# Reordering the start-up of a fused attention and two-layer kernel: one load, one attention pass and one product moved

## The chip, the cores and the metric

The kernel runs on one core of a Trainium2 chip. The metric is the device time of one execution in microseconds (us), as the median of several executions. All times come from runs whose state is "fast" unless the text says otherwise. A profiled execution of the same program gives the "span", from the first to the last instruction, which is about 1.7 us shorter than the device time.

Engine names as in the profile: PE is TensorE's matmuls, DVE VectorE, ACT ScalarE, POOL GpSimd, SP SyncE (SPq: the transfers that it issues).

## The reference, cut to what matters

```python
# q, k, v: (4, 8, 768, 64) f32; n_sink 4, window 64; heads 0, 2, 6 "retrieval"
scores = scale * np.matmul(q, k.transpose(0, 1, 3, 2))
causal = rel >= 0
stream_keep = causal & (is_sink | in_win)          # the other five heads
mask = full causal for retrieval heads, stream_keep for the others
a = exp(scores - max) / sum
x = (a @ v) with heads side by side                # (3072, 512)
h = x @ w_in                                       # 512 x 2048   "product 1"
g = np.maximum(0.01 * h, h)
return (g @ w_out).astype(np.float32)              # 2048 x 512   "product 2"
```

## The kernel before

The 3,072 tokens are worked through in eight chunks of 384 (CH), numbered n = 0 to 7. A chunk is loaded (q, k and v, cast to bf16 on the way), its q and k are transposed ("prep"), attention makes x, product 1 makes g in 16 blocks of four matmuls each, product 2 makes three output tiles in 15 portions of two to four matmuls. Each stage is a list of small functions ("slots"), and `merge` weaves two lists together. PSUM is the buffer in which TensorE leaves its results; its banks are taken by a tag: `bank("py", ...)`. The tags psS, ph and po have two banks each, py and pt one.

```python
def load(n, nms="kqv"):                 # L93: GpSimd issues, one piece per group of 128 tokens
    ...
            cast[nm, n] = rot.tile([128, 3, H, D], BF16, name=f"{nm}b", tag=f"{nm}b", bufs=2)
    ...
            nc.gpsimd.dma_start(out=o, in_=nat[nm][b, c, :, :, g])

def prep_pair(n, p, tag="pt", eng=("v", "v", "v")):
    ...
    pt = bank(tag, [128, 2, 4, 128], BF16)          # k and q of two heads in ONE bank
    for e, nm in enumerate("kq"):
        for g in range(3):
            nc.tensor.transpose(pt[:, e, g, :], cast[nm, n][:, g, 2 * p : 2 * p + 2, :], ident[:])   # L201
    ... # move(): VectorE tensor_copy (L206) for "v", ScalarE activation Copy (L208) for "a"
    for hh in range(2):
        r = slice(64 * hh, 64 * hh + 64)
        move(eng[hh], kt[i][r, p, hh, CH * c : CH * c + CH], pt[r, 0, 0:3, :])
        ...
    move(eng[2], qts[n][:, p, :], pt[:, 1, 0:3, :])

def prep_dma(n):                        # chunks 3 to 7: transposes by DMA, issued by SyncE
    ...
        nc.sync.dma_start_transpose(out=kt..., in_=kz[n % 2][:, g]...)            # L223
        nc.sync.dma_start_transpose(out=qts[n][:, :, t], in_=cast["q", n][:, g]...)   # L225

# Attention: scores L329, exp on ScalarE L334, times v L296; x: VectorE L402, transposes L411,
# copy of the transposed x out of bank "pt" on ScalarE L412
def in_slots(n, tags=("ph",)):
    def tick(t):                        # one of 16 blocks
        ph = bank(tags[t % len(tags)], [128, 512], FP32)
        for g in range(KG):
            nc.tensor.matmul(ph[:, 0:CH], lhsT=w_in_bf[...], rhs=xts[n][:, g, :], ...)      # L457
        nc.scalar.activation(out=gs[n][:, t, :], in_=ph[:, 0:CH], func=ACTF.Prelu, alpha=0.01)   # L459
    ...
def out_slots(n, tags=("py", "py", "py"), halves=False):
    ...                                 # matmuls with w_out L470, VectorE copy to o L475, store L476
```

The part of the program that the change touches, in the kernel before:

```python
for i in range(4):
    load_w("in", i)
load(1)
...
for i in range(4):
    load_w("out", i)
...                                     # attention of chunk 0
load(2)
in0 = in_slots(0, ("ph", "psS"))
run(in0[0:12])
for p in range(4):
    prep_pair(1, p, ("py", "pt")[p % 2])
    run(in0[12 + p : 13 + p])
...
a1 = Attention(1, po_tags=("po", "po", "po", "ph")).slots(order=[0, 2, 6, 1, 3, 4, 5, 7])
run(a1[0:4])
run(merge(out_slots(0, ("py", "ph", "py")), a1[4:] + [lambda: None] * 3))
...
in1 = in_slots(1)
run(in1[0:1])
run(merge(in1[1:] + out_slots(1, ("py", "ph", "py")), preps(2) + Attention(2).slots()))
```

The softmax here doesn't subtract the row's maximum and nothing guards it: scores larger than these inputs give would overflow.

## Time and profile before

The time before is 248.32 us, the median of three runs (247.95 to 249.04). The profiled execution, a run apart (248.99 us), has a span of 247.3 us.

| moment, from the TensorE timeline of the kernel before | us |
|---|---|
| product 1 of chunk 0 starts | 19.57 |
| first transposes of chunk 1 (first prep) | 27.62 |
| fifth portion of product 2 of chunk 0, after a wait for w_out | 44.99 |
| product 1 of chunk 1 starts | 57.68 |
| product 1 of chunk 2 starts | 87.64 |
| end | 247.3 |

A row of a timeline reads: start, duration, engine, line and operation, result<-operands, how many in one group, and in brackets how long the engine had been idle before it and whose result it had waited for. The page's rows of digits are tenths of busy time in 40 slices of the span, some 6.2 us each. The lines themselves stand in the prediction.

### The profile page before, as it was taken

The page shows a single profiled execution, that of the slowest core. Times are in us where ns is not written, and L with a number is a line of the kernel's source. Part 1 is how long each engine was busy: PE and PEld are TensorE (multiplying, and loading weights), DVE is VectorE, ACT ScalarE, POOL GpSimd, SP SyncE. Part 2 cuts the span into 40 slices and gives each one's busy share as a digit, 9 for nine tenths or more (in the row PEclk, how much of TensorE's full clock was granted, in tenths as well). Part 3 has the DMA queues.
Part 4 walks back from the last instruction along what each step waited for, and adds up shares of the span by engine and source line. Part 5 has one row for each costly group of instructions (what it writes and reads, how often), then busy time and mean ns, then how long its engine had stood idle before and what let it go on. Part 6 is the DMA issues. An engine that isn't in the chain of part 4 may idle for free.

```text
span 247.3 us, 4993 instructions
## 1 busy us (share of the span) xinstructions
PE 226.4 (92%) x1984; PEld 136.7 (55%) x1984; DVE 92.2 (37%) x261; ACT 130.4 (53%) x280; POOL 80.3 (32%) x108
## 2 busy tenths in 40 slices
PE   1778698898799999999999999999999999999994
PEld 0565354464465566656655666566556665555553
DVE  6883065274725423444421334224411352111121
ACT  2676436553484289865536675366436764333300
POOL 8993772679493804842810000000000000000000
PEclk9999979999999999999999999999999999999999
DMA  9999999999999999999999642197301212111012
GB/s 162 137 158 199 155 197 231 157 188 165 167 147 178 176 193 174 158 127 158 172 137 172 129 104 74 25 154 176 96 16 42 62 29 64 42 42 45 28 57 85
DMA packets 114858, 30.78 MB, mean 124 GB/s; under 512 B 105620, under 2 KB 110996, under 8 KB 114836
## 3 DMA queue, kind: packets, MB, share of 16 engines
q0 software_dynamic: 78304, 13.51, 79.7%
q1 hardware_dynamic: 36432, 16.95, 33.8%
q8 instruction: 15, 0.25, 0.4%
q14 instruction: 7, 0.06, 0.1%
q10 hardware_dynamic: 100, 0.02, 0.1%
HBM read 27.81 MB, written 6.29 MB: 138 GB/s over the span
## 4 chain that ended last, share of the span: by engine, by line
PE 76%; DMA 11%; POOL 6%; DVE 4%; issue 1%; ACT 1%; POOLq 0%
PE ph L457 27%; PE py L470 21%; PE po L296 6%; DMA w_out_bf<-in_moe_w_out_dram 6%; PE pt L470 6%; DMA w_in_bf<-in_moe_w_in_dram 5%; PE psS L329 4%; PE psS L470 4%; PE ph L470 3%; PE psS L365 2%; POOL va L93 2%; PE psS L309 2%; DVE o L475 1%; POOL qb L93 1%; POOL w_out_bf L102 1%
## 5 line engine op out<-in xcount | busy, mean ns | idle before, releaser
L457 PE MATMUL ph<-xt,w_in_bf 128*128 128x384 bf16 x480 | 97.6, 327 | 0.1
L459 ACT ACTIVATE g<-ph 128x384 bf16<-128x384 f32 x120 | 59.0, 492 | 59.4 <-PE ph L457 59.0
L470 PE MATMUL py<-w_out_bf,g 128*128 128x512 bf16 (+1 forms) x256 | 66.4, 372 | 1.3 <-DMA w_out_bf<-in_moe_w_out_dram 0.7
L457 PEld LDWEIGHTS <-w_in_bf 128*128 128x128 bf16 x512 | 46.4, 98 | 30.1 <-issue 1.0
L470 PEld LDWEIGHTS <-g 128*128 128x128 bf16 x400 | 35.4, 97 | 27.6 <-issue 2.3
L334 ACT ACTIVATE at<-psS 128x384 bf16<-128x384 f32 x81 | 39.0, 490 | 16.6 <-PE psS L329 15.1
L86 POOL DMA_DIRECT2D kz<-in_k_dram x30 | 22.5, 770 | 23.1 <-DMA kt<-kz 18.7
L475 DVE COPY o<-py 128x512 f32<-128x512 f32 (+1 forms) x16 | 10.8, 674 | 43.7 <-PE py L470 43.7
L329 PE MATMUL psS<-qt,kt 128*128 128x384 bf16 (+2 forms) x104 | 26.4, 295 | 0.6 <-ACT g L459 0.4
L93 POOL DMA_DIRECT2D qb<-in_q_dram x24 | 21.3, 903 | 13.3 <-DMA w_out_bf<-in_moe_w_out_dram 3.5
L93 POOL DMA_DIRECT2D va<-in_v_dram x24 | 21.2, 908 | 6.4 <-DMA w_out_bf<-in_moe_w_out_dram 3.3
L296 PE MATMUL po<-va,at 128*128 128x65 bf16 x237 | 20.4, 196 | 1.3 <-DVE at L340 1.0
L370 ACT ACTIVATE ats<-psS 128x384 bf16<-128x384 f32 x38 | 18.6, 493 | 5.5 <-PE psS L365 4.5
L296 PEld LDWEIGHTS <-at 128*128 128x128 bf16 x252 | 16.4, 100 | 8.0 <-DVE at L340 1.4
L402 DVE TENSOR_TENSOR xs<-po,linv 128x384 bf16<-128x384 f32 x30 | 16.7, 558 | 1.0
L470 PE MATMUL pt<-w_out_bf,g 128*128 128x512 bf16 x64 | 17.1, 379 | 0.0
L329 PEld LDWEIGHTS <-kt 128*128 128x128 bf16 x108 | 10.5, 100 | 9.9 <-issue 2.1
L340 DVE TENSOR_TENSOR at<-at,m_caus 128x128 bf16<-128x128 bf16 x24 | 5.3, 222 | 27.6 <-ACT at L334 27.3
L365 PEld LDWEIGHTS <-kt 128*128 128x128 bf16 x240 | 12.4, 101 | 5.4 <-issue 0.2
L296 PEld LDWEIGHTS <-ats 128*128 128x128 bf16 x240 | 11.5, 98 | 3.3
L365 PE MATMUL psS<-qt,kt 128*128 128x64 bf16 x228 | 13.1, 195 | 0.0
L338 DVE TENSOR_TENSOR at<-at,m_caus 128x256 bf16<-128x256 bf16 x24 | 7.0, 291 | 15.7 <-ACT at L334 15.5
(97 smaller groups left out, 194.0 us busy)
## 6 DMA issues: line engine op xcount, KB each, us to landing
out_dram<-o SPq DMA_DIRECT2D x23, 256.0 KB, 2.8
qb<-in_q_dram POOLq DMA_DIRECT2D x24, 128.0 KB, 6.0
va<-in_v_dram POOLq DMA_DIRECT2D x24, 128.0 KB, 7.3
w_in_bf<-in_moe_w_in_dram POOLq DMA_DIRECT2D x4, 512.0 KB, 9.0
w_out_bf<-in_moe_w_out_dram POOLq DMA_DIRECT2D x4, 512.0 KB, 12.0
kz<-in_k_dram POOLq DMA_DIRECT2D x30, 64.0 KB, 6.4
vb<-va SPq DMA_DIRECT2D x8, 195.0 KB, 5.8
vb<-va SPq DMA_DIRECT2D x6, 130.0 KB, 3.2
```

The costliest lines, as they stand in the source:

```text
L86: nc.gpsimd.dma_start(out=kz[n % 2][:, g, hh::2, D * hh : D * hh + D], in_=nat[nm][b, c, :, hh::2, g])
L93: nc.gpsimd.dma_start(out=o, in_=nat[nm][b, c, :, :, g])
L296: nc.tensor.matmul(o, lhsT=lhsT, rhs=rhs, start=first, stop=False, skip_group_check=True)
L329: nc.tensor.matmul(s[:, off : off + w], lhsT=kt[i][:, p, hh, 128 * kj : 128 * kj + 128], rhs=qts[n][:, p, lo:CH], start=(j == 0), stop=(j ...
L334: nc.scalar.activation(out=a[:, 0:off], in_=s[:, 0:off], func=ACTF.Exp, scale=SM)
L365: nc.tensor.matmul(s[:, 64 * m : 64 * m + 64], lhsT=kt[i][:, p, hh, k0 : k0 + 128], rhs=qts[n][:, p, 64 * m : 64 * m + 64], start=(m == 0) ...
L370: nc.scalar.activation(out=av_, in_=s[:, 0:CH].rearrange("p (j e f) -> p j e f", j=3, e=2), func=ACTF.Exp, scale=SM)
L402: nc.vector.tensor_tensor(xs[:], po[:, :, :, 0:D], linv.to_broadcast([128, 3, 2, D]), op=ALU.mult)
L457: nc.tensor.matmul(ph[:, 0:CH], lhsT=w_in_bf[:, g, 128 * t : 128 * t + 128], rhs=xts[n][:, g, :], start=(g == 0), stop=(g == KG - 1))
L459: nc.scalar.activation(out=gs[n][:, t, :], in_=ph[:, 0:CH], func=ACTF.Prelu, alpha=0.01)
L470: nc.tensor.matmul(py[n][:, 0 : c1 - c0], lhsT=gs[n][:, ng, 128 * tt : 128 * tt + 128], rhs=w_out_bf[:, ng, c0:c1], start=(ng == 0), stop= ...
L475: nc.vector.tensor_copy(o[:, 0 : c1 - c0], py[n][:, 0 : c1 - c0])
```

## The change

The intent is to fill the holes of the first third. Chunk 1 is loaded ahead of the last quarter of w_in, so that its attention can start right after twelve of sixteen blocks of product 1; that attention runs before product 2 instead of inside it; and the second half of product 2 is woven into product 1 of the next chunk. In chunk 1's preps the q copy goes to ScalarE ("vva").

```diff
--- before.py
+++ after.py
@@ -452,7 +452,7 @@
         def tick(t):
             if t == 0:
                 gs[n] = rot.tile([128, NG, CH], BF16, name="g", tag="g", bufs=2)
-            ph = bank(tags[t % len(tags)], [128, 512], FP32)
+            ph = bank(tags[t % len(tags)] if t < 12 else "ph", [128, 512], FP32)
             for g in range(KG):
                 nc.tensor.matmul(ph[:, 0:CH], lhsT=w_in_bf[:, g, 128 * t : 128 * t + 128],
                                  rhs=xts[n][:, g, :], start=(g == 0), stop=(g == KG - 1))
@@ -518,9 +518,10 @@
     load(0, "v")
     load_vb0()
     masks()
-    for i in range(4):
+    for i in range(3):
         load_w("in", i)
     load(1)
+    load_w("in", 3)
     for a in ats:
         nc.vector.memset(a[:, :, 1:3, :], 0.0)
     for i in range(4):
@@ -535,28 +536,33 @@
     run(a0[6:])
     zeros(0, 1)
     nc.vector.memset(ksink[1][:], 0.0)
+    zeros(1, 0)
+    zeros_k(1)
+    zeros_k(0)
     load(2)
+    load(3)
     in0 = in_slots(0, ("ph", "psS"))
     run(in0[0:12])
-    for p in range(4):
-        prep_pair(1, p, ("py", "pt")[p % 2])
-        run(in0[12 + p : 13 + p])
+
+    for j, p in enumerate((0, 1, 3, 2)):
+        prep_pair(1, p, ("py", "pt")[j % 2], "vva")
+        if j == 1:
+            a1 = Attention(1, po_tags=("po", "po", "po", "ph")).slots(order=[0, 2, 6, 1, 3, 4, 5, 7])
+        if j > 0:
+            run(a1[j - 1 : j])
     v_shift(1, nc.sync)
-    zeros(1, 0)
-    zeros_k(1)
-    load(3)
-    zeros_k(0)
-
-    a1 = Attention(1, po_tags=("po", "po", "po", "ph")).slots(order=[0, 2, 6, 1, 3, 4, 5, 7])
-    run(a1[0:4])
-    run(merge(out_slots(0, ("py", "ph", "py")), a1[4:] + [lambda: None] * 3))
+    run(a1[3:8])
+    run(merge(in0[12:], a1[8:16]))
+    out0 = out_slots(0, ("py", "py", "py"))
+    run(merge(out0[0:8], a1[16:] + [lambda: None] * 4))
     v_shift(2, nc.sync)
     load(4)
     prep_dma(3)
     v_shift(3, nc.sync)
-    in1 = in_slots(1)
-    run(in1[0:1])
-    run(merge(in1[1:] + out_slots(1, ("py", "ph", "py")), preps(2) + Attention(2).slots()))
+    x = merge(in_slots(1), out0[8:])
+    run(x[:8])
+    a2 = [lambda j=j: prep_pair(2, j, ("pt", "psS")[j % 2]) for j in range(4)] + Attention(2).slots()
+    run(merge(x[8:] + out_slots(1, ("ph", "py", "ph")), a2))
     outs = []
 
     for n in range(2, NCH):
```

## The prediction

> **What bounds the kernel now.** I read the page first, for the busy row and the slices.
>
> ```profile
> span 247.3 us, 4993 instructions
> PE 226.4 (92%) x1984; PEld 136.7 (55%) x1984; DVE 92.2 (37%) x261; ACT 130.4 (53%) x280; POOL 80.3 (32%) x108
> PE   1778698898799999999999999999999999999994
> PEclk9999979999999999999999999999999999999999
> DMA  9999999999999999999999642197301212111012
> ```
>
> TensorE is the bound, but its digits are full only from the twelfth slice (68 us) on; before that there are holes, while DMA is full. Busy time hides part of them, because overlapped matmul records are counted with their tails. So I worked out the pure work from the instruction order: every matmul at the spacing the trace shows (384 columns 0.163 us: four take 0.65; 512 columns 0.216 us: four take 0.86; 128 columns 0.056; 65 columns 0.030). All 1,984 sum to 214.7 us, so 32.6 us of the span is not work. Up to the start of chunk 2's product 1 (87.48 us) the work is 62.0 us and the loss 25.5; after it the loss is 7 us. The change touches only the stretch from 27.62 to 87.48 us: 48.2 us of work in 59.9, a loss of 11.6. The TensorE timeline shows the first hole:
>
> ```profile
> 27.62 0.28 PE L201 MATMUL py<-ident,kb 128*128 128x128 bf16 x2
> 28.42 0.23 PE L201 MATMUL py<-ident,kb 128*128 128x128 bf16 x1 [0.52 <-DMA kb<-in_k_dram]
> 29.33 0.23 PE L201 MATMUL py<-ident,qb 128*128 128x128 bf16 x1 [0.68 <-DMA qb<-in_q_dram]
> 30.24 0.23 PE L201 MATMUL py<-ident,qb 128*128 128x128 bf16 x1 [0.67 <-DMA qb<-in_q_dram]
> 31.09 0.29 PE L201 MATMUL py<-ident,qb 128*128 128x128 bf16 x1 [0.62 <-DMA qb<-in_q_dram]
> 31.17 1.49 PE L457 MATMUL ph<-xt,w_in_bf 128*128 128x384 bf16 x4
> ```
>
> Chunk 1's k and q land one piece per 0.9 us and TensorE takes each as it comes. Then from 31.17 four 384-column matmuls need 1.28 us instead of 0.65: the clock is halved until about 34.4. Later holes of the same view:
>
> ```profile
> 40.60 0.27 PE L296 MATMUL po<-va,at 128*128 128x65 bf16 x3 [0.97 <-DVE at L340]
> 44.99 1.02 PE L470 MATMUL py<-w_out_bf,g 128*128 128x512 bf16 x4 [0.74 <-DMA w_out_bf<-in_moe_w_out_dram]
> 61.24 0.34 PE L201 MATMUL pt<-ident,kb 128*128 128x128 bf16 x3 [1.10 <-DVE qt L206]
> 63.46 0.34 PE L201 MATMUL pt<-ident,kb 128*128 128x128 bf16 x3 [0.41 <-DVE qt L206]
> 65.55 0.34 PE L201 MATMUL pt<-ident,kb 128*128 128x128 bf16 x3 [0.94 <-DVE qt L206]
> ```
>
> The chain that ended last says what sets this stretch: two transfers, the last quarter of w_in and then the last quarter of w_out, landing at 25.5 and 44.95 us.
>
> ```profile
> 13.77 11.72 DMA w_in_bf<-in_moe_w_in_dram
> 30.48 14.47 DMA w_out_bf<-in_moe_w_out_dram
> 44.99 1.02 PE py L470 x4
> ```
>
> **What the Trainium skill says.** "DMA: Bandwidth & Descriptors", "Issuing engines are not separate DMA queues": all DMAs run on the same 16 engines, whoever issues them. So moving a load does not make bytes faster; it decides who waits. The trace agrees: DMA is at 9 in the first 22 slices. The same page, "SWDGE vs HWDGE vs iDMA": a casting DMA can only come from GpSimd, so f32-to-bf16 loads of k, q, v and weights stand in one issue order; the trace has them all on POOL. "TensorE: Matmul & The Clock Gate", Part 1: after an idle window of about 3.4 us the clock is halved, and a busy window restores it. Here the slow stretch 31.1 to 34.4 us follows 3.2 us in which TensorE did six transposes. The table "Back-to-back issue gap" of that page has N/2.4 + 2.5 ns; the 0.65 and 0.86 us above agree.
>
> **The change, part by part.**
>
> (a) Load order. The quarters of w_in land about 2.8 us apart (5.5, 9.0 and 11.7 us least, median and most to landing, issues 0.75 us apart). One quarter leaves the place ahead of chunk 1: its last q piece lands at 31.1 - 2.8 = 28.3 us, its v at 31.3, and the fourth quarter of w_in at about 34.0. The bytes ahead of w_out don't change, so its quarters still land at about 36.2, 40.1, 42.6 and 44.95 us (read from which GpSimd issue waited for each: no more than eight are outstanding).
>
> (b) Stretch from 27.62. Preps of chunk 1 stall until about 28.4 instead of 31.1. TensorE is half busy in that window instead of an eighth, so I expect no halved clock. The four preps are then paced by VectorE (two k copies of 0.36 each, 0.72 a pair; the q copy goes to ScalarE): four pairs, about 3 us, to 31.5, with attention-1 slots in between. Slots 3 to 7 run at ScalarE's pace (0.43 us an exp) to 33.5. The last four blocks of product 1 (0.65 each) with eight slots take some 5 us, to 38.5; the fourth w_in quarter is there just in time.
>
> (c) Product 2 of chunk 0 with slots 16 to 25. The third, fourth and fifth portions need w_out quarters that land at 42.6 and 44.95. My pace gets TensorE to the third portion at about 41.2, so it waits, and the fifth starts at 45.0, as before. What is different is what is done by then. Before, at 45.0 only twelve of 26 attention-1 slots were done and eleven of fifteen product-2 portions were left, 12.7 us more to the end of attention 1. After, only the two last x transposes are left beside product 2.
>
> (d) All portions now share the single bank py. Between the fifth and sixth portion lies only 0.33 us of transposes while VectorE evacuates py (0.69 us plus handoffs): about 0.6 us of new stall. So: 45.0 + 0.86 (four matmuls) + 0.33 + 0.6 + 1.94 (nine matmuls) = 48.75.
>
> (e) Chunk 1's product 1 with the rest of product 2, then its product 2, chunk 2's preps and attention 2: 31.65 us of work by the sum over the order. Preps of chunk 2 now alternate two banks (pt, psS) and sit between longer blocks; VectorE needs 1.48 to 1.66 us for each, 6.3 in all, and the first score that needs the last psS buffer comes about 6.7 us after the first prep. The 2.45 us of prep waits above shrink to some 0.3. I keep the 0.8 us of small losses that this stretch has today. End: 48.75 + 31.65 + 0.3 + 0.8 = 81.5 against 87.48.
>
> (f) After that the instruction streams are the same. Sum: 6.0 us off the span, none of it given back; I take 0.2 off for a weave that I can't see fully. 248.3 - 5.8 = 242.5 us.
>
> **Rivals.**
>
> 1. w_out is the wall, and the weave only waits longer in front of it. For: TensorE reaches it idle, and the landing doesn't move. Against: independent of that, 4.9 us of attention 1 moves ahead of the wall. If it held entirely, only the prep banks' 2 us would be won: 246.3. A w_out that lands 1 us later makes 243.5.
>
> 2. ScalarE becomes the pace. Attention 1 now has little matmul work beside it: from 28.5 to the third portion ScalarE has 28 activations at 0.38 us, 10.6 us, so it ends at 39.1, three and a half under the 42.6 of the wall. If scores, masks and the single free ph buffer add 2 us, nothing is lost; 4 us would lose 1 to 2 (244).
>
> 3. Transfers push back later. SyncE now has chunk 3's k and q transposes in front of four of chunk 0 and 1's outputs, and chunk 4's q load waits for those transposes. For: three o buffers only. Against: the transposes took 12 us before (60.25 to 72.4), can start at about 54.5 when v of chunk 2 has landed, and the first o that must be reused comes at about 75. If it blocks, VectorE blocks with it and 1 to 3 us are lost.
>
> 4. The half clock comes back in the preps' window. Then the attention slots of 31 to 34 us take 0.5 us instead of 0.26, ahead of the wall: 0.5 us lost at most.
>
> **Range and chances.** Rivals 1 (the mild form), 3 and 4 each take 0.5 to 2 us; nothing in sight gives more than 1 us beyond the sum. So 242.5, and 241.0 to 245.0 eight times in ten. The 2% line is at 243.4, 0.9 us from my value, with an error that I put at 1.5 us: faster 0.70, within 2% 0.28, slower 0.02.
>
> **What would show it.** Right if: the last q piece of chunk 1 is waited for at about 28.3; the PEclk digit of 7 is gone; the wait for w_out at 45.0 stays, with attention 1's streams before it; the chain's long pieces are again w_in or chunk 1's load, then w_out; a wait of TensorE on VectorE's o copy (about 0.6 us) at 46; the waits of preps on VectorE drop from 2.45 us to under 1; chunk 2's product 1 starts at about 81.5. Wrong if w_out lands later than 46, if TensorE reaches it later than 45.5, if prep or score waits of more than 2 us stand between 49 and 82, or if the stretch from there to the end is not 160 us long.

## The result, and the profile after

The changed kernel takes 244.97 us (median of four runs, 244.49 to 245.99), the kernel before 248.13 in the same rounds (247.90 to 249.04). The ratio is 0.9871, with a 95% interval of 0.9830 to 0.9913: 1.3% faster. A ratio here is the mean time of one kernel's fast runs over that of the other's fast runs of the same rounds, so it is not quite the ratio of the medians quoted. The time lies inside the predicted range; the favoured class, faster by over 2%, did not come.

The page of the kernel after, its span, busy and slice rows:

```profile
span 243.0 us, 4966 instructions
...
PE 224.3 (92%) x1957; PEld 136.6 (56%) x1984; DVE 90.1 (37%) x257; ACT 131.6 (54%) x284; POOL 80.4 (33%) x108
...
PE   1778879989999999999999999999999999999994
...
PEclk9997999999999999999999999999999999999999
DMA  9999999999999999999999941676210111111112
```

The work is the same (1,957 of the 1,984 matmuls are recorded). TensorE's row is full from the tenth slice, not the twelfth, so the change did close holes. The digit 7 of PEclk has not gone: it moved from the sixth slice to the fourth.

The TensorE timeline of the kernel after, its main moments:

```profile
28.81 0.33 PE L201 MATMUL py<-ident,kb 128*128 128x128 bf16 x3
...
30.71 0.32 PE L329 MATMUL psS<-qt,kt 128*128 128x384 bf16 x1 [1.06 <-ACT qt L208]
...
33.14 0.32 PE L329 MATMUL psS<-qt,kt 128*128 128x384 bf16 x1 [0.89 <-ACT at L334]
...
35.78 0.32 PE L329 MATMUL psS<-qt,kt 128*128 128x384 bf16 x1
...
36.47 0.81 PE L457 MATMUL ph<-xt,w_in_bf 128*128 128x384 bf16 x4
...
46.92 1.67 PE L470 MATMUL py<-w_out_bf,g 128*128 128x512 bf16 x7
...
49.34 0.33 PE L411 MATMUL pt<-ident,xs 128*128 128x128 bf16 x3 [0.58 <-DVE o L475]
...
51.45 0.81 PE L457 MATMUL ph<-xt,w_in_bf 128*128 128x384 bf16 x4
```

Chunk 1's q and k are there when TensorE asks for them. Then two new waits appear, both on ScalarE: 1.06 us for a q copy and 0.89 for an exp. There is no wait for w_out: the row of seven matmuls holds portions four and five, and the fifth starts three matmuls (0.65 us) after 46.92, at 47.57, when the last quarter, landing at 44.95, has been there for 2.6 us. Ahead of the last x transpose stands a wait of 0.58 us, put down to VectorE's copy of the output tile.

| TensorE reaches | before | predicted | after |
|---|---|---|---|
| first prep of chunk 1 (wait for the load over) | 27.62 (31.1) | 28.4 | 28.81 |
| slot 8 of attention 1, which opens the weave with the last four blocks (the first block) | (31.17) | 33.5 | 35.78 (36.47) |
| product 2, first portion | 38.65 | 38.5 | 41.57 |
| product 2, fifth portion | 44.99 | 45.0 | 47.57 |
| product 1 of chunk 1 | 57.68 | 48.75 | 51.45 |
| product 1 of chunk 2 | 87.64 | 81.5 (for a score 0.16 earlier) | 83.40 |
| end of the span | 247.3 | 241.3 (6.0 off) | 243.0 |

Most of the loss against the prediction arises between two lines of this table: 0.4 us late at the first prep, 2.3 late at slot 8 (numbered from 0; its score is the row at 35.78). The weave with the four blocks then takes 5.8 us (35.78 to 41.57) instead of some 5, which makes 3.1, and from there on the loss stays below that. What happens between the first prep and slot 8 shows in VectorE's timeline:

```profile
29.35 0.72 DVE L206 COPY kt<-py 64x384 bf16<-64x384 bf16 x2 [4.69 <-PE py L201]
```

and in ScalarE's:

```profile
30.17 0.49 ACT L208 ACTIVATE qt<-py 128x384 bf16<-128x384 bf16 x1 [0.66 <-DVE kt L206]
30.92 0.49 ACT L208 ACTIVATE qt<-pt 128x384 bf16<-128x384 bf16 x1 [0.26 <-DVE kt L206]
...
33.37 3.70 ACT L334 ACTIVATE at<-psS 128x384 bf16<-128x384 f32 x8
```

The q part of the bank had been written by 29.3, but ScalarE starts its copy at 30.17, after VectorE's second k copy of the same bank has ended at 30.07, and the profile says that it waited for that copy. The chain that ended last, which ran through the two weight transfers before, now goes the same way:

```profile
28.98 0.35 PE py L201 x6
29.35 0.35 DVE kt L206
29.71 0.37 DVE kt L206
30.17 0.50 ACT qt L208
```

### The profile page after: what moved, and what is told of

Its sections match the earlier page's. It is cut to its first block, busy times and chain, and to the rows that moved or that the text cites. A ratio compares the mean times of both kernels' runs of the same rounds, so it can differ in the third digit from the quotient of the medians.

```text
span 243.0 us, 4966 instructions
## 1 busy us (share of the span) xinstructions
PE 224.3 (92%) x1957; PEld 136.6 (56%) x1984; DVE 90.1 (37%) x257; ACT 131.6 (54%) x284; POOL 80.4 (33%) x108
## 3 DMA queue, kind: packets, MB, share of 16 engines
q1 hardware_dynamic: 36432, 16.95, 35.2%
## 4 chain that ended last, share of the span: by engine, by line
PE 86%; DVE 5%; ACT 3%; DMA 2%; issue 2%; POOL 1%; DVEq 0%; ACTq 0%; POOLq 0%
PE ph L457 31%; PE py L470 22%; PE po L296 6%; PE pt L470 6%; PE psS L329 6%; PE psS L470 4%; PE ph L470 3%; PE psS L365 2%; DMA qb<-in_q_dram 2%; PE psS L457 2%; DVE o L475 2%; PE psS L309 2%; DVE xs L402 1%; ACT at L334 1%; PE pt L411 1%
## 5 line engine op out<-in xcount | busy, mean ns | idle before, releaser
L457 PE MATMUL ph<-xt,w_in_bf 128*128 128x384 bf16 x488 | 99.8, 328 | 0.0
L459 ACT ACTIVATE g<-ph 128x384 bf16<-128x384 f32 x122 | 60.1, 492 | 57.5 <-PE ph L457 56.8
L470 PE MATMUL py<-w_out_bf,g 128*128 128x512 bf16 (+1 forms) x238 | 63.0, 371 | 1.5
L470 PEld LDWEIGHTS <-g 128*128 128x128 bf16 x400 | 36.0, 97 | 28.3 <-issue 1.4
L470 PE MATMUL pt<-w_out_bf,g 128*128 128x512 bf16 x57 | 15.7, 379 | 0.4
L340 DVE TENSOR_TENSOR at<-at,m_caus 128x128 bf16<-128x128 bf16 x24 | 5.4, 224 | 28.5 <-ACT at L334 28.3
L329 PEld LDWEIGHTS <-kt 128*128 128x128 bf16 x108 | 10.6, 100 | 9.0 <-issue 1.6
L365 PEld LDWEIGHTS <-kt 128*128 128x128 bf16 x240 | 11.7, 98 | 5.2 <-issue 0.2
L412 ACT ACTIVATE xt<-pt 128x384 bf16<-128x384 bf16 x14 | 6.9, 494 | 10.7 <-PE pt L411 10.7
```

Of the source, the lines that this page charges most:

```text
L329: nc.tensor.matmul(s[:, off : off + w], lhsT=kt[i][:, p, hh, 128 * kj : 128 * kj + 128], rhs=qts[n][:, p, lo:CH], start=(j == 0), stop=(j ...
L365: nc.tensor.matmul(s[:, 64 * m : 64 * m + 64], lhsT=kt[i][:, p, hh, k0 : k0 + 128], rhs=qts[n][:, p, 64 * m : 64 * m + 64], start=(m == 0) ...
L457: nc.tensor.matmul(ph[:, 0:CH], lhsT=w_in_bf[:, g, 128 * t : 128 * t + 128], rhs=xts[n][:, g, :], start=(g == 0), stop=(g == KG - 1))
L470: nc.tensor.matmul(py[n][:, 0 : c1 - c0], lhsT=gs[n][:, ng, 128 * tt : 128 * tt + 128], rhs=w_out_bf[:, ng, c0:c1], start=(ng == 0), stop= ...
```

## The experiments

My theory after the result: the q copy on ScalarE cannot run beside VectorE's k copies, because both read one PSUM bank; so k, k and q go one after the other, the first score waits, ScalarE falls behind by some 1.5 us, and the exps that follow queue behind the q copies. Rivals: the holes could be filled with other TensorE work anyway; the two score buffers or the single banks py and pt are the cause; or the difference is only the position of a stretch of half clock (some 3.4 us in which the profile has a granted TensorE clock of 0.5). The kernels below are edits of the kernel after, unless said otherwise. The runs of the kernel before on their chip: 248.85 us for load_only, weave_only, all_vector and fill_holes; 248.77 for after_again, split_banks, second_bank and four_scores; 248.83 for x_bank, split_x and split_x_scores; and 248.72 for split_x_q3.

### load_only: the kernel before, with the new order of loads alone

```diff
-    for i in range(4):
+    for i in range(3):
         load_w("in", i)
     load(1)
+    load_w("in", 3)
```

> The kernel before with the new load order alone. Theory (TensorE executes in order, and the first block of product 1 that needs the fourth quarter of w_in stands right behind the first prep): no gain. The q wait at 31.1 us moves to 28.3, but that block then waits for the quarter until about 34, with a halved clock behind it, and the fifth portion of product 2 comes 0 to 2 us later than the 45.0 of now: ratio to before 1.000 to 1.008. Rival (the earlier chunk-1 load is itself the gain): 2 to 2.8 us faster, ratio 0.989 to 0.992.

Measured: ratio 1.0059 (1.0039 to 1.0078), 250.18 us. The TensorE timeline of this run has one long wait instead of four short ones:

```profile
33.52 1.46 PE L457 MATMUL ph<-xt,w_in_bf 128*128 128x384 bf16 x4 [4.67 <-DMA w_in_bf<-in_moe_w_in_dram]
```

In the old program the earlier chunk 1 is worth nothing: product 1's last blocks still come next, and the last quarter of w_in lands at 33.5 (the prediction had about 34.0).

### weave_only: the kernel after, with the old order of loads

```diff
-    for i in range(3):
+    for i in range(4):
         load_w("in", i)
     load(1)
-    load_w("in", 3)
```

> The changed kernel with the old load order. Theory (in the changed kernel TensorE reaches the last w_out quarter at 47.6, later than its landing at 45, so a delay ahead of it is paid in full): preps start when q lands at 31.1 instead of 28.8, with a halved clock behind, so 2 to 3.5 us slower than the changed kernel, ratio to before 0.995 to 1.002. Rival (the landing of w_out is the wall and hides a delay): under 1 us slower than the changed kernel, ratio to before at most 0.991.

Measured: ratio 0.9970 (0.9948 to 0.9992), 248.09 us. TensorE waits for the same q pieces as before the change, the last of them at 30.97:

```profile
30.97 0.23 PE L201 MATMUL py<-ident,qb 128*128 128x128 bf16 x1 [0.62 <-DMA qb<-in_q_dram]
```

The new order of work alone gives 0.3%, the new order of loads alone costs 0.6%, the two together gain 1.3%. Most of the gain needs both.

### all_vector: the q copies of chunk 1 back on VectorE

```diff
-        prep_pair(1, p, ("py", "pt")[j % 2], "vva")
+        prep_pair(1, p, ("py", "pt")[j % 2], "vvv")
```

> The changed kernel with chunk 1's q copies given back to VectorE. Theory (the q copy on ScalarE starts only when VectorE has left the same PSUM bank, so it is no parallel work, and it takes ScalarE's time ahead of the exps, which set the pace up to 41 us): 0.5 to 1.5 us faster than the changed kernel, first score at about 30.5 instead of 30.7 us, first block of product 1 of the last four at about 35.5 instead of 36.5. Rival (VectorE sets the pace of the preps): 0.5 to 1.5 us slower, as VectorE then has 1.1 instead of 0.72 us for each pair.

Measured: ratio 0.9814 (0.9789 to 0.9840), 244.12 us, against 0.9871 and 0.9872 for the kernel after (after_again, below): 0.6% faster. Its TensorE timeline:

```profile
29.93 0.34 PE L329 MATMUL psS<-qt,kt 128*128 128x384 bf16 x1 [0.86 <-DVE qt L206]
...
34.71 0.81 PE L457 MATMUL ph<-xt,w_in_bf 128*128 128x384 bf16 x4
```

Three copies one after the other on one engine are no slower than two on one and one on the other: the first score waits 0.86 instead of 1.06 us (a q copy takes 0.36 us on VectorE, 0.49 on ScalarE). This agrees with the copies having been serial all the time. What is gained is ScalarE: without four q copies the exps finish earlier. The profiled run also had no stretch of half clock, so its 1.76 us at the last blocks (34.71 against 36.47) is not all due to the edit; the timed runs are the measure.

### fill_holes: two blocks of product 1 kept back for the waits in the preps

```diff
-    run(in0[0:12])
+    run(in0[0:10])
 ...
         prep_pair(1, p, ("py", "pt")[j % 2], "vva")
+        if j < 2:
+            run(in0[10 + j : 11 + j])
```

> The changed kernel with two of the first twelve blocks of product 1 held back and put after the first and second prep. Theory (TensorE idles there while PSUM is evacuated, 1.06 us before the first score): 1.3 us of work moves into waits of about 1.9 us, so 0.7 to 1.3 us faster than the changed kernel, and the fifth portion of product 2 starts at about 46.5. Rival (ScalarE's chain of exps alone sets the pace from 31 to 41 us): the two activations of these blocks are added to it, and nothing is won, 0.3 us either way.

Measured: ratio 0.9885 (0.9855 to 0.9916), 245.75 us: no gain. The first prep now comes at 26.62, but the timeline shows TensorE waiting 0.68 and 0.60 us for q pieces that land up to 28.6. The blocks were moved into a hole, and a hole of about the same size opened ahead of it. Besides, the two blocks put two more leaky-ReLU evictions between the q copies and exps on ScalarE, which was late already, and this profile has its half clock at 34 to 37.4 us and a wait of 1.32 us at 105.60 us (for the q of chunk 4, see split_x). Which of these ate the gain isn't told apart; that filling holes of TensorE with ready work is not enough by itself is.

### after_again: the kernel after, unchanged, for its spread

> The changed kernel once more, unchanged, as a partner on the same chip and for the spread of its clock: ratio to before 0.985 to 0.990. If the halved clock that its first trace shows from 19.5 to 22.5 us (1.2 us lost) belongs to the kernel, this trace shows it again at the same place; if it depends on where a free-running window falls, it is somewhere else or absent.

Measured: ratio 0.9872 (0.9857 to 0.9887), 245.55 us, so the result repeats. Its profile differs in one point: the half clock lies at 35.2 to 38.6 us, not at 19.1 to 22.6. The first score starts at 30.11 instead of 30.71, so the early half clock cost 0.6 us there; TensorE then loses as much and more later, and chunk 2's product 1 starts at 84.25. The wait of 1.06 us for the q copy is the same to the digit, wherever the half clock lies.

### split_banks: q transposed into a bank of its own

```diff
-    def prep_pair(n, p, tag="pt", eng=("v", "v", "v")):
+    def prep_pair(n, p, tag="pt", eng=("v", "v", "v"), qtag=None):
 ...
+        pq = bank(qtag, [128, 2, 4, 128], BF16) if qtag else pt
-                nc.tensor.transpose(pt[:, e, g, :], cast[nm, n][:, g, 2 * p : 2 * p + 2, :], ident[:])
+                nc.tensor.transpose((pt, pq)[e][:, e, g, :], cast[nm, n][:, g, 2 * p : 2 * p + 2, :], ident[:])
-        move(eng[2], qts[n][:, p, :], pt[:, 1, 0:3, :])
+        move(eng[2], qts[n][:, p, :], pq[:, 1, 0:3, :])
 ...
-        prep_pair(1, p, ("py", "pt")[j % 2], "vva")
+        prep_pair(1, p, ("py", "pt")[j % 2], "vva", qtag="ph")
```

The engines, the copies and their sizes are those of the kernel after; only the bank of the q half changes.

> The changed kernel with chunk 1's q transposes in a bank of their own (ph), k's where they were. Theory (in the changed kernel ScalarE's q copy starts only when VectorE has left the same bank, at 30.17 after copies that end at 30.07): the q copy now starts beside VectorE's copies, the first score comes about 0.7 us earlier, 0.5 to 1.0 us faster in all. Rival (ScalarE's own load is the pace, not the order of the two copies): under 0.3 us.

Measured: ratio 0.9779 (0.9754 to 0.9804), 243.31 us: 2.2% faster than before and 2.2 us below after_again, more than the 0.5 to 1.0 us that I had expected. Its ScalarE timeline:

```profile
29.57 0.87 ACT L209 ACTIVATE qt<-ph 128x384 bf16<-128x384 bf16 x2
```

and its TensorE timeline:

```profile
28.98 0.33 PE L202 MATMUL py<-ident,kb 128*128 128x128 bf16 x3
...
30.10 0.32 PE L330 MATMUL psS<-qt,kt 128*128 128x384 bf16 x1 [0.29 <-ACT qt L209]
...
34.34 0.32 PE L330 MATMUL psS<-qt,kt 128*128 128x384 bf16 x1
...
35.03 0.81 PE L458 MATMUL ph<-xt,w_in_bf 128*128 128x384 bf16 x4
```

Two q copies follow each other from 29.57, while VectorE is still copying k of the first pair (29.35 to 30.07): they run side by side now. The wait for q is 0.29 us instead of 1.06, and the last blocks of product 1 start at 35.03 instead of 36.47, 1.44 us earlier, in a profile whose half clock lies where that of the kernel after lay.

Counted from the first prep to slot 8, which takes out where the clock had put the start, the kernel after needs 6.97 us and second_bank (below, same preps) 6.96, this run 5.36 (28.98 to 34.34) and split_x_q3 (below, same preps as here) 5.37: the bank is worth 1.6 us, and the prediction had 5.1 for the stretch. This is the direct test, and it settles that sharing the bank held the q copy back. The edit also makes k's banks free sooner and takes the two of ph for q; that isn't told apart, but for the first pair no bank had to come free, and its score comes 0.6 us earlier (30.10 against 30.71). The rest of the 2.2 us is open and may be in part the clock: after_again was granted 0.986 to 0.993 in its four runs, split_banks 0.992 to 1.000 in five.

The run is also 0.35% below all_vector, as two engines at work side by side should be against one, but those two ran in different calls and their intervals overlap.

### second_bank: the second output tile of chunk 0 in another bank

```diff
-    out0 = out_slots(0, ("py", "py", "py"))
+    out0 = out_slots(0, ("py", "psS", "py"))
```

> The changed kernel with the second tile of chunk 0's product 2 in a psS bank instead of py. Theory (TensorE waits 0.58 us for VectorE to empty the one py bank between the first and the second tile, and that wait is on the path): the wait disappears, 0.5 to 0.7 us faster than the changed kernel. Rival (what follows is gated by something else, such as the x transposes): no change.

Measured: ratio 0.9864 (0.9839 to 0.9889), 245.12 us: no change against after_again. The wait is still there, to the digit:

```profile
49.37 0.33 PE L411 MATMUL pt<-ident,xs 128*128 128x128 bf16 x3 [0.58 <-DVE o L475]
49.54 2.10 PE L470 MATMUL psS<-w_out_bf,g 128*128 128x512 bf16 x9
```

So the 0.58 us are not the wait for py to be emptied, although the profile names that copy and I had predicted just that. What waits is an x transpose into pt. In the kernel after, pt is emptied by a ScalarE copy from 48.80 to 49.29, ending 0.05 us before the transpose starts; the VectorE copy ended at about the same time (48.63 and 0.69 us long) and was named.

### x_bank: the last of four x transposes in psS instead of pt

```diff
-            a1 = Attention(1, po_tags=("po", "po", "po", "ph")).slots(order=[0, 2, 6, 1, 3, 4, 5, 7])
+            a1 = Attention(1, po_tags=("po", "po", "po", "ph"), x_tags=("pt", "pt", "pt", "psS")).slots(order=[0, 2, 6, 1, 3, 4, 5, 7])
```

> The changed kernel with the last x transposes of attention 1 in a psS bank instead of pt. After the bank of product 2 was changed without effect, theory: the 0.58 us wait before those transposes, put down to VectorE's o copy, is a wait for ScalarE to empty the single pt bank of the transposes before (its copy ends at 49.29, the transposes start at 49.34). Then the wait disappears here and a wait for the single py bank of 0.3 to 0.5 us stands in its place: 0 to 0.5 us faster. Rival (the transposes wait for VectorE's x scaling): the 0.58 us stay.

Measured: ratio 0.9857 (0.9827 to 0.9886), 245.34 us, not to be told from the kernel after. The TensorE timeline tells more:

```profile
48.27 0.33 PE L411 MATMUL psS<-ident,xs 128*128 128x128 bf16 x3
...
49.04 2.10 PE L470 MATMUL py<-w_out_bf,g 128*128 128x512 bf16 x9 [0.45 <-DVE o L475]
```

The wait ahead of the transpose is gone, so pt it was; and 0.45 us of waiting now stand at the next portion of product 2, this time really for py. The two single banks are emptied at almost the same time, so freeing one of them gains 0.13 us.

### four_scores: four buffers for the scores instead of two

```diff
-            a1 = Attention(1, po_tags=("po", "po", "po", "ph")).slots(order=[0, 2, 6, 1, 3, 4, 5, 7])
+            a1 = Attention(1, ("psS", "ph"), po_tags=("po", "po", "po", "ph")).slots(order=[0, 2, 6, 1, 3, 4, 5, 7])
```

(and the two extra banks only for the first nine scores, until product 1 needs them)

> The changed kernel with the first nine scores of attention 1 in four buffers (psS and ph in turn) instead of the two of psS. Theory (between 33.4 and 37.1 us eight exps take 3.70 us, 0.46 each, where ScalarE does them at 0.37 when the next score lies ready; the rest is the round trip exp, score, exp through two buffers): 0.5 to 0.9 us faster. Rival (ScalarE's throughput is the pace): under 0.2 us. Risk: ph is shared with the last blocks of product 1.

Measured: ratio 0.9852 (0.9825 to 0.9879), 244.66 us: 0.2% below after_again, with intervals that overlap widely. The wait for the q copy stays at 1.06 us. More score buffers are no cure while ScalarE is late. This and the x_bank run say nothing finer than that.

### split_x and split_x_scores: the edits together

split_x is split_banks with x_bank, and split_x_scores adds four_scores.

> The version with q transposes in their own bank, and the last x transposes in psS as well. Theory: both gains add up, ratio to before 0.975 to 0.979. In a trace without a halved clock before 28 us the fifth portion of product 2 is reached at about 45.0, where the last quarter of w_out lands. Rival (w_out now takes over): the second gain is lost in a wait for w_out that the trace names, ratio as with the split banks alone, 0.978.

> Split banks, x bank and the four score buffers together. Theory (the landing of w_out at about 44.9 us is the next wall): TensorE reaches the fifth portion of product 2 before it and the trace shows a wait for w_out of 0.2 to 1 us, so the score buffers add at most 0.3 us to the version before, ratio 0.974 to 0.979. Rival (no wall): another 0.3 to 0.7 us, ratio under 0.975 and no wait for w_out.

Measured: split_x 0.9846 (0.9823 to 0.9870), 244.84 us; split_x_scores 0.9806 (0.9778 to 0.9834), 243.89 us. Both were to be better than split_banks and neither is: split_x is 0.7% worse, and split_x_scores can't be told from split_banks (the intervals overlap). Yet in split_x's profile chunk 2's product 1 starts at 81.06 us, earlier than in any other run (83.40 in the kernel after, 81.95 in split_banks). That lead over split_banks is the clock, not the edit: this profile has no half clock ahead, that of split_banks has one, and so has that of split_x_q3 (below), where the same program but for one buffer arrives at 82.10. What was ahead is given back afterwards, in its TensorE timeline:

```profile
102.88 0.32 PE L330 MATMUL psS<-qt,kt 128*128 128x384 bf16 x1 [1.81 <-DMA qt<-qb]
...
129.54 0.32 PE L458 MATMUL ph<-xt,w_in_bf 128*128 128x384 bf16 x1 [0.67 <-DMA xt<-xs]
```

The transposed q of chunk 4 lands at 102.8 us. TensorE, which came for it at 103.24 in the kernel after without waiting, comes 1.81 us too early. A wait for w_out, which could have been the next wall, is in none of these profiles; even in split_x, where the fifth portion starts at 45.07, the weights have landed at 44.7.

### split_x_q3: split_x with a third buffer for the loaded q

Why is chunk 4's q late? The change moved the load of chunk 3 up, and with two buffers chunk 4's q load must now wait until chunk 3's q has been transposed. GpSimd's timeline of the kernel before:

```profile
66.36 2.64 POOL L93 DMA_DIRECT2D qb<-in_q_dram  x3 [3.33 <-PE pt L201]
```

and of the kernel after:

```profile
73.96 2.64 POOL L93 DMA_DIRECT2D qb<-in_q_dram  x3 [9.94 <-DMA qt<-qb]
```

So I gave q a third buffer:

```diff
-                cast[nm, n] = rot.tile([128, 3, H, D], BF16, name=f"{nm}b", tag=f"{nm}b", bufs=2)
+                cast[nm, n] = rot.tile([128, 3, H, D], BF16, name=f"{nm}b", tag=f"{nm}b", bufs=3 if nm == "q" else 2)
```

> This is split_x with a third buffer for the loaded q. Theory: split_x had gained 2.6 us by the start of chunk 2's product 1 (81.06 against 83.40 us) and gave it back later, because chunk 4's q load at 73.8 us waits for chunk 3's transposes to leave the buffer that it overwrites; then the load goes out at about 66 us, the 1.8 us wait for q at 102.9 us and most of the 0.67 us wait for x at 129.5 us go, the stretch after the start of chunk 2's product 1 is 160 us again instead of 162.4, and the ratio to before is 0.972 to 0.978. Rival: the transposes are late because SyncE and the transfers are the pace, not this load; then the waits stay and the ratio is 0.983 to 0.987, as split_x's.

Measured: ratio 0.9829 (0.9802 to 0.9857) over five fast runs, 244.63 us; a sixth run, slow, is left out. That is at the edge of what the rival gave and outside of the theory's range. The load did move: its first piece is issued at 66.47 us.

```profile
66.47 0.89 POOL L93 DMA_DIRECT2D qb<-in_q_dram  x1 [0.71 <-PE ph L458]
```

But SyncE's queue of transfers, in the same run, shows what the load does not change:

```profile
70.65 12.54 SPq L477 DMA_DIRECT2D out_dram<-o  x5
83.36 1.28 SPq L224 DMA_TRANSPOSE kt<-kz  x1
...
94.99 1.30 SPq L226 DMA_TRANSPOSE qt<-qb  x1
```

and TensorE gets its q at the same time:

```profile
102.73 0.32 PE L330 MATMUL psS<-qt,kt 128*128 128x384 bf16 x1 [0.62 <-DMA qt<-qb]
```

Chunk 4's transposes stand on SyncE behind the stores of chunk 1's output, the last of which is issued at 82.86, so they begin at 83.36 whatever happened to the load, and q lands at 102.7 instead of 102.8. The wait shrank from 1.81 to 0.62 us only because TensorE came later (this profile has the early half clock). The rival holds in its main point: this load is not the pace. That the order on SyncE is, the queue suggests, and no run tests it: what an earlier place of the transposes would give was not run.

The fastest of all kernels is split_banks. Its TensorE comes for chunk 4's q at 101.81 and does not wait: SyncE issued the last transpose of chunk 4's q at 94.92, nearly as in split_x_q3 (94.99). The trace has no landing for this transfer, but TensorE's starts bound it: at most 6.9 us after the issue here, 7.7 in split_x_q3, and 9.4 in split_x, which issued it earliest (93.46). So the place in the queue alone doesn't decide it either. Why a landing takes so different a time isn't settled.

## Why the prediction was right or wrong

The time lies in the range, 2.5 us above the predicted value; the favoured class was wrong. By the prediction's own steps:

**(a) Load order: right.** The last quarter of w_in landed at 33.5 (about 34.0 predicted, load_only). Chunk 1's last q piece was waited for at 28.49 in after_again (28.3 predicted); in the profiled run TensorE came for it later. w_out's last quarter landed at 44.95, as predicted.

**(b) The step that failed.** The prediction says: "The four preps are then paced by VectorE (two k copies of 0.36 each, 0.72 a pair; the q copy goes to ScalarE): four pairs, about 3 us, to 31.5". It took the q copy for parallel work that costs the path nothing. In the runs it is serial: 0.72 us of VectorE, then 0.50 of ScalarE, and only then is the bank free for the next pair. VectorE ended its last copy at 32.88, not 31.5, and slot 8, which was to begin at 33.5, began at 35.78: ScalarE had the q copies and the exps to do in one row, and the exps came at 3.70 / 8 = 0.46 us each, not 0.43.

The mechanism is confirmed by split_banks, which moves only the q half to another bank. Of the 2.3 us, 0.4 are the late start, 1.6 the shared bank (6.97 against 5.36 us from the first prep to slot 8) and 0.3 stay unexplained. In split_x, with the q half in its own bank and no half clock ahead, slot 8 begins at 33.27. The weave with the four blocks was sized too small as well, 5.0 us for 5.8, and it takes 5.8 in split_x too, so the bank has no part in that.

The Trainium skill has a rule that fits, in "PSUM — Partial Sum Buffer", section "PSUM bank collisions raise a hardware error": two engines must not touch one bank and quadrant (32 partitions) at once, reads included, and the compiler's scheduler, the page says, adds a dependency between any two such instructions. The trace agrees that one waits for the other (0.66 us, ACT on DVE). That a collision would raise an error, no run here shows; nor whether the wait hangs on the bank or on the tile, since split_banks changes both. I had read the pages on transfers and on TensorE, not this one, and the answer stood in it.

The late start is the clock: the early half clock has TensorE at the first prep at 28.81, where after_again, without it, is there at 27.72 and waits for q until 28.49. At the first score the two differ by 0.6 us (30.71 and 30.11).

**(c) The w_out wall: wrong, for the reason of (b).** The prediction had TensorE waiting for w_out until 45.0. It arrived at the fifth portion at 47.57, past the 45.5 that the prediction had named as a sign of being wrong. By its own figures the wall would have swallowed some 1.4 us of delay (third portion reached at 41.2, its weights there at 42.6); TensorE came to the third portion at 45.14, so what was left of the delay, 2.6 us at the fifth portion, went into the total. Rival 1 therefore didn't happen, and the chain that ended last no longer holds the two weight transfers that I expected in it.

**(d) The single bank: the size right, the bank wrong.** A stall of 0.6 us was predicted at py; 0.58 us were measured at pt. From the fifth portion to the start of chunk 1's product 1 the prediction has 3.75 us and the run 3.88.

**(e) The stretch of chunk 1: better than predicted.** 83.40 - 51.45 = 31.95 us against 32.75 (31.65 of work, 0.3 and 0.8 of losses). Between 51 and 84 us the timeline of the kernel after has no wait of TensorE, where the kernel before had 2.45 us for its preps.

**(f) The rest: right.** 243.0 - 83.40 = 159.6 us, and 247.3 - 87.64 = 159.7 before.

**The rivals.** Rival 2 (ScalarE as the pace) named the right engine but put its end at 39.1, under a wall of 42.6; it counted activations and left out that a copy on ScalarE must wait for VectorE. Its bad branch, 4 us more and 244 us in all, came nearest: the third portion was 3.9 us late (45.14 for 41.2). Rival 3 (transfers push back) did not cost anything in the kernel after, but it was only hidden: TensorE came for chunk 4's q at 103.24 without a wait; in split_x it came at 101.07 and waited 1.81 us. Rival 4 named the half clock, in the wrong place: the preps' window stayed at full clock in the profiled run, and product 1 of chunk 0 got it.

**The sum.** Predicted 6.0 us off the span, measured 4.3: (b) and the clock cost 2.7 up to chunk 1's product 1 (51.45 against 48.75), and (e) and (f) gave 1.0 back. That the time fell inside the range is owed to the width of the range and to that 1.0, not to the account of (b) and (c). The medians differ by 3.2 us only, since the profiled execution of the kernel before was a slow one (248.99 us), and the prediction had taken its loss from that one.

## What to carry to other kernels

Here two engines shared work only once they read different PSUM banks: when a tile's copies are split between VectorE and ScalarE, give each engine its own bank, or leave all copies on one engine, and look in the profile whether they overlap. When a chain of copies gates the next score, count it as a sum, and look for who is named in the wait of the second copy. And before an early stage is sped up, look how much slack the later transfers have: a profile that shows no wait needn't have much. 2.2 us earlier at the same score, TensorE waited for 1.81.

## What the Trainium skill lacked or had wrong

- "TensorE: Matmul & The Clock Gate", Part 1, says that the clock is halved after an idle window of about 3.4 us and that the window is free-running. The second agrees with the runs: one kernel had its half clock at 19.1 to 22.6 us in one profile and at 35.2 to 38.6 in another, and all_vector had none. How idle a window must be is not said, and it need not be empty: in after_again the 3.4 us ahead of the halving had TensorE busy for 2.17 us by the profile, 64%, and in the kernel after 1.74 us, 51%.
- "PSUM — Partial Sum Buffer" has the rule on banks but no figure for what it costs a kernel: here the second reader started 0.66 us later, TensorE waited 1.06 us for it, and a bank of its own for q was worth 1.6 us in the profiles and 2.2 of 245 in the timed runs.
- No page that I found says that a wait can name the wrong instruction when two end together: the 0.58 us put down to VectorE's copy was ScalarE's emptying of pt, as second_bank (still 0.58) and x_bank (gone) show.
